# The opening of a fused convolution and MLP: first tile convolved on TensorE by tap diagonals, VectorE's convolution issued ahead by a time budget

## The chip, the cores and the metric

One core of a Trainium2 chip runs the whole kernel. The metric is the device time of one execution in microseconds; the median over the runs counts. TensorE (PE in the profile) multiplies, ScalarE (ACT) applies the silu, VectorE (DVE) convolves and copies results out of PSUM, GpSimd (POOL) and SyncE (SP) issue DMAs.

## What is computed

A causal depthwise convolution of 7 taps over the sequence, whose taps are a softmax over 7 weights of each of 8 heads, feeds a two-layer MLP with a silu that has its own beta for every hidden unit:

```python
batch, seq, d_model = (8, 4096, 192)      # 32768 tokens
kernel_size, n_heads, d_ff = 7, 8, 2048
w = softmax(weight, axis=-1)              # (8, 7)
x_pad = concatenate([zeros((B, 6, D)), x], axis=1)
out = einsum('hk,bskhg->bshg', w, windows of 7 of x_pad, 24 channels a head)
h = out @ w_in                            # (32768, 192) @ (192, 2048)
g = h * (1.0 / (1.0 + exp(-beta * h)))
result = g @ w_out                        # (32768, 2048) @ (2048, 192), float32
```

## The kernel before

The tokens are two streams (`NS = 2`) of 16384 each, four sequences a stream. Stream 0 lies in partitions 0 to 63 of every activation tile, stream 1 in 64 to 127, and the 192 channels are `NK = 3` groups of 64. A step takes the same tokens of both streams. The steps are 128, 128 and 256 tokens (the first tile of 512), and then 31 full tiles of 512.

In a step, `mm1` (L251) makes one of the 16 chunks of 128 hidden units: six matmuls of 64 rows (three channel groups, two streams) into a `ph` tile of PSUM, of which there are two, and one ScalarE activation (L259) that writes `g = silu(beta h)` for both streams. So w_in must lie in both halves of the partitions: `load_w_in` brings each column to one half by a casting DMA from POOL, and `copy_w_in` copies it to the other by a DMA from SP. `mm2` (L285) multiplies the step before: its matmuls of 64 x 192 are set among the `mm1` of this step by `mm2_plan`, gather in two `po` tiles of PSUM, and `store` (L298) copies a finished pair to `o_sb` on VectorE (L301) and writes it out by a DMA from SP. w_out is divided by beta on POOL (L207), because g holds beta h times the sigmoid.

The tokens arrive transposed. `load_x` (L89) brings 128 tokens of one stream a time by a casting DMA from POOL (256 in all), and `transpose_x` (L99) turns a block by a DMA transpose on SP. `conv_ops` (L210) makes for step i+1 a list of a halo copy and 21 VectorE operations (7 taps, 3 groups), one pass over 128 x n each (L229, L231), from the transposed `xt` through a float32 `acc` to the bf16 `xc` that `mm1` reads. The order of the work is written out by hand, each instruction pinned to program order on its engine; the loop takes two of those operations after each `mm1`:

```python
for u in range(NF):
    mm1(i, u)
    for t in plan[u]:
        mm2(i - 1, *t)
    for op in conv[:2]:
        op()
    conv = conv[2:]
```

Step 0 has a path of its own: VectorE multiplies the 128 tokens by each tap (`xw`, L168), and 42 matmuls with a shifted identity add them up (L185). Steps 1 and 2 take the common path.

Of the kernel before, what the change touches and what calls it, by code (L numbers as in the profile page):

```python
# [10 lines left out]
FP32 = mybir.dt.float32  # L11
BF16 = mybir.dt.bfloat16
# [6 lines left out]
def kernel(  # L19
# [9 lines left out]
    nc = tc.nc  # L29
# [4 lines left out]
    group = D // H  # L34
# [3 lines left out]
    NK = D // 64  # L38
    NS = 2
    TS = B * S // NS  # L40
    TILE = 512

# [8 lines left out]
    xbf_pool = ctx.enter_context(tc.tile_pool(name="xbf", bufs=3))  # L51
# [8 lines left out]

    steps = [(0, 128), (128, 128), (256, 256)]
    steps += [(t, TILE) for t in range(TILE, TS, TILE)]
    n_steps = len(steps)


    x0 = consts.tile([128, NS, D], FP32, name="x0")
    pin(nc.sync.dma_start(out=x0, in_=xs[:, 0:128, :].rearrange("s p d -> p s d")))
    wbc = consts.tile([128, H, K], FP32, name="wbc")
    pin(nc.sync.dma_start(out=wbc, in_=weight.rearrange("h k -> (h k)").partition_broadcast(128)))
    beta16 = consts.tile([NF, 128], FP32, name="beta16")  # L70
    pin(nc.sync.dma_start(out=beta16, in_=moe_beta.rearrange("(c p) -> c p", p=128)))

    w_in_s = consts.tile([128, NK, F], BF16, name="w_in_s")
    w_in_v = moe_w_in.rearrange("(k c) f -> c k f", c=64)
# [4 lines left out]
    def load_w_in(half, f0, f1):  # L79
        pin(nc.gpsimd.dma_start(out=w_in_s[64 * half:64 * half + 64, :, f0:f1], in_=w_in_v[:, :, f0:f1]))  # L80

    def copy_w_in(half, f0, f1):
        o = 1 - half
        pin(nc.sync.dma_start(out=w_in_s[64 * o:64 * o + 64, :, f0:f1],
                              in_=w_in_s[64 * half:64 * half + 64, :, f0:f1]))

    xbf_of, xt_of = {}, {}

    def load_x(j, b0=0, b1=4):  # L89
        if j not in xbf_of:  # L90
            xbf_of[j] = xbf_pool.tile([128, 4, NK, NS, 64], BF16, name="x_bf")
        t = xbf_of[j]
        for b in range(b0, b1):
            for s in range(NS):
                src = xs[s, TILE * j + 128 * b:TILE * j + 128 * (b + 1), :]
                pin(nc.gpsimd.dma_start(out=t[:, b, :, s, :],  # L96
                                        in_=src.rearrange("p (k c) -> p k c", c=64)))

    def transpose_x(j, b0=0, b1=4):  # L99
        if j not in xt_of:  # L100
            xt_of[j] = xt_pool.tile([128, NK, LEAD + TILE], BF16, name="xt")
        for b in range(b0, b1):
            c = LEAD + 128 * b
            pin(nc.sync.dma_start_transpose(
                out=xt_of[j][:, :, c:c + 128],
                in_=xbf_of[j][:, b, :, :, :].rearrange("p k s c -> p (k s c)")))


    zeros = consts.tile([128, TILE], BF16, name="zeros")
# [7 lines left out]
    load_w_in(0, 0, 512)  # L117
    load_w_in(1, 0, 512)
    shift = consts.tile([128, 128 + PAD], BF16, name="shift")
    pin(nc.gpsimd.memset(shift, 0.0))  # L120
    pin(nc.gpsimd.affine_select(out=shift, in_=shift, compare_op=ALU.not_equal, fill=1.0,
                                base=PAD, pattern=[[-1, 128 + PAD]], channel_multiplier=1))
    id16 = consts.tile([NF, NF], FP32, name="id16")
    pin(nc.gpsimd.memset(id16, 0.0))
    pin(nc.gpsimd.affine_select(out=id16, in_=id16, compare_op=ALU.not_equal, fill=1.0,
                                base=0, pattern=[[-1, NF]], channel_multiplier=1))
    load_x(0, 0, 4)
    mask = consts.tile([128, NK, H], FP32, name="mask")
    pin(nc.gpsimd.memset(mask, 1.0))
    for s in range(NS):  # L130
        m = mask[64 * s:64 * s + 64, :, :]
        pin(nc.gpsimd.affine_select(out=m, in_=m, compare_op=ALU.is_ge, fill=0.0, base=0,  # L132
                                    pattern=[[64, NK], [-group, H]], channel_multiplier=1))
        pin(nc.gpsimd.affine_select(out=m, in_=m, compare_op=ALU.is_ge, fill=0.0, base=group - 1,  # L134
                                    pattern=[[-64, NK], [group, H]], channel_multiplier=-1))
    load_w_in(0, 512, 1024)
    load_w_in(1, 1024, 1536)
    load_w_in(0, 1536, 2048)
    load_x(1)

    for c in range(0, NF, 4):
        pin(nc.sync.dma_start(out=w_out_f[:, c:c + 4, :], in_=w_out_v[:, c:c + 4, :]))  # L142
        if c == 0:
            transpose_x(0, 0, 2)
            copy_w_in(0, 512, 1024)
        if c == 4:
            copy_w_in(1, 1024, 1536)
            transpose_x(0, 2, 4)
        if c == 8:
            copy_w_in(0, 1536, 2048)  # L150


    mx = consts.tile([128, H], FP32, name="mx")
    pin(nc.vector.tensor_reduce(out=mx, in_=wbc, axis=AX.X, op=ALU.max))
    pin(nc.vector.tensor_tensor(wbc, wbc, mx[:, :, None].to_broadcast([128, H, K]), ALU.subtract))
    pin(nc.scalar.activation(wbc, wbc, AF.Exp))
    pin(nc.scalar.activation(scrap, one, AF.Silu))
    sm = consts.tile([128, H], FP32, name="sm")
    pin(nc.vector.tensor_reduce(out=sm, in_=wbc, axis=AX.X, op=ALU.add))
    rs = consts.tile([128, H], FP32, name="rs")  # L160
    pin(nc.vector.reciprocal(rs, sm))
    taps = consts.tile([128, H, K], FP32, name="taps")
    pin(nc.vector.tensor_tensor(taps, wbc, rs[:, :, None].to_broadcast([128, H, K]), ALU.mult))


    xw = consts.tile([128, K, NS, D], BF16, name="xw")
    for k in range(K):
        pin(nc.vector.tensor_tensor(  # L168
            xw[:, k, :, :].rearrange("p s (h c) -> p s h c", c=group),
            x0.rearrange("p s (h c) -> p s h c", c=group),  # L170
            taps[:, None, :, k:k + 1].to_broadcast([128, NS, H, group]),
            ALU.mult))

    warm = psum_h.tile([128, 2, TILE], FP32, name="ph")
    for i in range(8):
        pin(nc.tensor.matmul(warm[:, i % 2, :], zeros[:, 0:128], zeros, start=True, stop=True))  # L176
    bps = psum_h.tile([128, 2, TILE], FP32, name="ph")
    pin(nc.tensor.transpose(bps[:, 0, 0:NF], beta16, id16))
    cva = psum_o.tile([128, 2, TILE], FP32, name="po")
    cvb = psum_o.tile([128, 2, TILE], FP32, name="po")  # L180
    cv = [cva[:, 0, 0:128], cva[:, 1, 0:128], cvb[:, 0, 0:128]]
    for k in range(K):
        for kk in range(NK):
            for s in range(NS):
                pin(nc.tensor.matmul(cv[kk][64 * s:64 * s + 64, :], xw[:, k, s, 64 * kk:64 * kk + 64],  # L185
                                     shift[:, k:k + 128], start=(k == 0), stop=(k == K - 1)))
    xc_of = {}
    xc_of[0] = xc_pool.tile([128, NK, TILE], BF16, name="xc")
    for kk in range(NK):
        pin(nc.scalar.activation(xc_of[0][:, kk, 0:128], cv[kk], AF.Copy))  # L190

    beta = consts.tile([128, NF], FP32, name="beta")
    pin(nc.vector.tensor_copy(beta, bps[:, 0, 0:NF]))
    rbeta = consts.tile([128, NF], FP32, name="rbeta")
    pin(nc.vector.reciprocal(rbeta, beta))

    tmp3 = consts.tile([128, NK, K, H], FP32, name="tmp3")
    for kk in range(NK):
        pin(nc.vector.tensor_tensor(tmp3[:, kk, :, :],
                                    mask[:, kk:kk + 1, :].to_broadcast([128, K, H]),  # L200
                                    taps.rearrange("p h k -> p k h"), ALU.mult))
    taps3 = consts.tile([128, NK, K], FP32, name="taps3")
    pin(nc.vector.tensor_reduce(out=taps3, in_=tmp3, axis=AX.X, op=ALU.add))


    for c in range(NF):
        pin(nc.gpsimd.tensor_scalar_mul(w_out_s[:, c, :], w_out_f[:, c, :], rbeta[:, c:c + 1]))  # L207


    def conv_ops(i):  # L210
        t0, n = steps[i]
        j, c0 = t0 // TILE, t0 % TILE
        ops = []

        def halo():
            xt = xt_of[j]
            if t0 % S == 0 or t0 == 128:
                pin(nc.vector.memset(xt[:, :, LEAD - PAD:LEAD], 0.0))
            elif c0 == 0:
                pin(nc.vector.tensor_copy(xt[:, :, LEAD - PAD:LEAD], xt_of[j - 1][:, :, TILE + LEAD - PAD:]))  # L220

        def tap(kk, k):
            xt, xc = xt_of[j], xc_of[i]
            acc = accs[i]
            src = xt[:, kk, LEAD - PAD + c0 + k:LEAD - PAD + c0 + k + n]
            w = taps3[:, kk, k:k + 1]
            a = acc[:, kk, 0:n]
            if k == 0:
# [6 lines left out]
        def begin():  # L235
            xc_of[i] = xc_pool.tile([128, NK, TILE], BF16, name="xc")
            accs[i] = acc_pool.tile([128, NK, TILE], FP32, name="acc")
            if c0 == 0 or t0 == 128:
                halo()

        ops.append(begin)
        for k in range(K):
            for kk in range(NK):
                ops.append(lambda kk=kk, k=k: tap(kk, k))
# [133 lines left out]
```

## Time and profile before

| | |
|---|---|
| three runs, median (lowest to highest) | 715.44 us (715.34 to 716.18) |
| the profiled execution | 712.91 us, of which its span is 711.2 us |
| PE busy, share of the span | 687.7 us, 97% |
| ACT, DVE, POOL busy | 578.8, 502.2, 218.2 us |
| mm1 matmuls (L257), mm2 matmuls (L293) | 432.7 us of 3264, 422.4 us of 7936 |
| mean granted TensorE clock | 0.999 |
| DMA over the span | 55.38 MB, 78 GB/s |

The profile is of one execution, so its own time is the one to compare with its span; the median stands 2.5 us above it. Busy times overlap between engines and do not add up to the span, and matmul busy time is that of pipelined instructions. A row of a timeline gives its start, its duration, engine, line, operation, output and input, and in brackets the idle time before it with what ended it.

### The profile page before, as it was taken

To read this page: it belongs to the slowest core of one execution; us is meant where nothing else is said; L and a number is where in the kernel's file an instruction comes from. 1 tells how busy PE (TensorE), PEld (TensorE's weight loads), DVE (VectorE), ACT (ScalarE), POOL (GpSimd) and SP (SyncE) were. 2 spreads that over 40 slices of the span, in tenths; PEclk is the share of its full clock that TensorE was granted. 3 is DMA by queue.
4 is the path that set the end of the run, shared out by engine and by line. 5 is a ranking of instruction groups with operands and counts; after the bars stand their busy time and mean duration, and the time that the engine had idled before them with its cause. 6 is when DMAs were issued, how large, how long until landed. Compare 5 with 4: busy or idle time off the path is not lost.

```text
span 711.2 us, 25346 instructions
## 1 busy us (share of the span) xinstructions
PE 687.7 (97%) x11379; PEld 524.5 (74%) x11379; DVE 502.2 (71%) x877; ACT 578.8 (81%) x552; POOL 218.2 (31%) x290
## 2 busy tenths in 40 slices
PE   5589999999999999999999999999999999999998
PEld 2466777777777777777777777777777777777777
DVE  4779776677687667678667768766776876676702
ACT  3489888888888888888888888888888888888882
POOL 9997332223333113333212333321233330000000
PEclk9999999999999999999999999999999999999999
DMA  9999554455555445555445555544555553221012
GB/s 132 149 95 96 81 88 69 72 84 79 75 80 87 69 73 85 75 72 87 79 71 78 74 74 81 88 71 71 83 80 74 80 85 64 58 62 52 28 44 68
DMA packets 194861, 55.38 MB, mean 78 GB/s; under 512 B 158128, under 2 KB 194752, under 8 KB 194752
## 3 DMA queue, kind: packets, MB, share of 16 engines
q0 software_dynamic: 103440, 13.58, 30.6%
q1 hardware_dynamic: 91312, 40.17, 22.3%
q8 instruction: 89, 1.46, 0.9%
q14 instruction: 20, 0.16, 0.1%
HBM read 28.94 MB, written 25.17 MB: 76 GB/s over the span
## 4 chain that ended last, share of the span: by engine, by line
PE 93%; POOL 2%; DMA 2%; DVE 2%; issue 0%; ACT 0%; SPq 0%; DVEq 0%; POOLq 0%
PE ph L257 46%; PE po L293 46%; PE po L316 2%; DVE acc L231 1%; POOL x_bf L96 1%; DMA w_in_s<-w_in_s 1%; DMA x_bf<-in_x_dram 1%; POOL w_in_s L80 0%; ACT g L259 0%; DVE xc L231 0%; DVE acc L229 0%; SPq L142 0%; POOL mask L132 0%; POOL mask L134 0%; DVE o_sb L320 0%
## 5 line engine op out<-in xcount | busy, mean ns | idle before, releaser
L259 ACT ACTIVATE g<-ph,beta 128x1024 bf16<-128x1024 f32 (+2 forms) x544 | 574.9, 1064 | 111.8 <-PE ph L257 107.4
L257 PE MATMUL ph<-xc,w_in_s 64*128 64x512 bf16 (+2 forms) x3264 | 432.7, 367 | 17.0 <-DMA w_in_s<-w_in_s 9.4
L293 PEld LDWEIGHTS <-g 64*128 64x128 bf16 x7936 | 359.6, 94 | 101.5
L293 PE MATMUL po<-w_out_s,g 64*128 64x192 bf16 x7936 | 422.4, 243 | 0.0
L231 DVE SCALAR_TENSOR_TENSOR acc<-xt,taps,acc 128x512 f32<-128x512 bf16 (+2 forms) x495 | 326.7, 727 | 0.0
L96 POOL DMA_DIRECT2D x_bf<-in_x_dram x256 | 197.5, 774 | 366.7 <-DMA xt<-x_bf 349.4
L257 PEld LDWEIGHTS <-w_in_s 64*128 64x128 bf16 x3264 | 168.2, 96 | 74.6 <-DMA w_in_s<-w_in_s 10.5
L301 DVE COPY o_sb<-po 128x384 f32<-128x384 f32 x124 | 68.9, 556 | 183.5 <-PE po L293 183.5
L231 DVE SCALAR_TENSOR_TENSOR xc<-xt,taps,acc 128x512 bf16<-128x512 bf16 (+2 forms) x99 | 66.5, 727 | 0.0
L229 DVE TENSOR_SCALAR acc<-xt,taps 128x512 f32<-128x512 bf16 (+2 forms) x99 | 41.8, 481 | 9.2 <-DMA xt<-x_bf 8.1
L207 POOL TENSOR_SCALAR w_out_s<-w_out_f,rbeta 128x192 bf16<-128x192 f32 x16 | 15.6, 992 | 0.1
L316 PE MATMUL po<-w_out_s,g 128*128 128x192 bf16 x128 | 10.7, 246 | 0.0
L316 PEld LDWEIGHTS <-g 128*128 128x128 bf16 x128 | 10.5, 98 | 0.2 <-issue 0.2
L320 DVE COPY o_sb<-po 128x192 f32<-128x192 f32 x8 | 2.9, 358 | 7.6 <-PE po L316 7.6
L176 PE MATMUL ph<-zeros 128*128 128x512 bf16 x8 | 3.6, 631 | 1.2 <-DVE one L112 1.2
L220 DVE COPY xt<-xt 128x18 bf16<-128x18 bf16 x28 | 4.6, 166 | 0.0
L185 PE MATMUL po<-shift,xw 128*64 128x128 bf16 x42 | 3.3, 314 | 1.2 <-DVE xw L168 1.2
L185 PEld LDWEIGHTS <-xw 128*64 128x64 bf16 x42 | 2.0, 152 | 2.4 <-DVE xw L168 2.4
L80 POOL DMA_DIRECT2D w_in_s<-in_moe_w_in_dram x5 | 3.3, 665 | 0.8 <-POOLq L362 0.8
L168 DVE TENSOR_TENSOR xw<-x,taps 128x384 bf16<-128x384 f32 x7 | 3.4, 553 | 0.0
L176 PEld LDWEIGHTS <-zeros 128*128 128x128 bf16 x8 | 1.0, 140 | 2.9 <-issue 1.7
L190 ACT ACTIVATE xc<-po 128x128 bf16<-128x128 f32 x3 | 0.6, 278 | 3.1 <-PE po L185 3.1
(30 smaller groups left out, 8.8 us busy)
## 6 DMA issues: line engine op xcount, KB each, us to landing
out_dram<-o_sb SPq DMA_DIRECT2D x124, 192.0 KB, 2.3
x_bf<-in_x_dram POOLq DMA_DIRECT2D x256, 48.0 KB, 3.1
xt<-x_bf SPq DMA_TRANSPOSE x128, 2.3
w_out_f<-in_moe_w_out_dram SPq DMA_DIRECT2D x4, 384.0 KB, 6.7
w_in_s<-in_moe_w_in_dram POOLq DMA_DIRECT2D x5, 192.0 KB, 5.5
out_dram<-o_sb SPq DMA_DIRECT2D x8, 96.0 KB, 1.6
w_in_s<-w_in_s SPq DMA_DIRECT2D x3, 192.0 KB, 6.8
x<-in_x_dram SPq DMA_DIRECT2D x1, 192.0 KB, 2.6
```

Of the source, the lines that this page charges most:

```text
L96: pin(nc.gpsimd.dma_start(out=t[:, b, :, s, :], in_=src.rearrange("p (k c) -> p k c", c=64)))
L176: pin(nc.tensor.matmul(warm[:, i % 2, :], zeros[:, 0:128], zeros, start=True, stop=True))
L185: pin(nc.tensor.matmul(cv[kk][64 * s:64 * s + 64, :], xw[:, k, s, 64 * kk:64 * kk + 64], shift[:, k:k + 128], start=(k == 0), stop=(k == K ...
L207: pin(nc.gpsimd.tensor_scalar_mul(w_out_s[:, c, :], w_out_f[:, c, :], rbeta[:, c:c + 1]))
L220: pin(nc.vector.tensor_copy(xt[:, :, LEAD - PAD:LEAD], xt_of[j - 1][:, :, TILE + LEAD - PAD:]))
L229: pin(nc.vector.tensor_scalar_mul(a, src, w))
L231: pin(nc.vector.scalar_tensor_tensor(out=xc[:, kk, 0:n] if k == K - 1 else a, in0=src, scalar=w, in1=a, op0=ALU.mult, op1=ALU.add))
L257: pin(nc.tensor.matmul(ph[:, s, 0:n], w_in_s[r, kk, ts(fc, 128)], xc_of[i][r, kk, 0:n], start=(kk == 0), stop=(kk == NK - 1)))
L259: pin(nc.scalar.activation(g_of[i][:, fc, :, 0:n], ph[:, :, 0:n], AF.Silu, scale=beta[:, fc:fc + 1]))
L293: pin(nc.tensor.matmul(po[:, q, 0:D], g_of[i][r, fc, s, ts(b, 128)], w_out_s[r, fc, :], start=(phase == 0 and fc == 0), stop=(phase == 1 a ...
L301: pin(nc.vector.tensor_copy(o_sb, po[:, :, 0:D]))
L316: pin(nc.tensor.matmul(po[:, 0, 0:D], g_of[i][:, fc, s, ts(b, 128)], w_out_s[:, fc, :], start=(fc == 0), stop=(fc == NF - 1)))
```

## The change

The tail (`last`) and `mm1` and `mm2` of the full steps stay as they are. These parts differ:

- **Channels.** Channel c now belongs to group c mod 3 (`(q k)` instead of `(k c)`), so the 64 lanes of every group carry the same heads, 8 lanes each, and one tap scalar a partition serves all three groups (`tapn`).
- **Taps.** They are loaded as 8 x 7 and spread over 128 partitions by a matmul with a 0/1 selector; the softmax is done there, and its division goes into the scaling of the results (`rsum`).
- **First tile.** Its four blocks of 128 tokens are loaded as float32, transposed on TensorE, and convolved there: seven diagonal matrices, one a tap, are the weights, in float32r. The diagonal matrix of a half is repeated over all 128 output columns, so both halves of the partitions get the channels of one stream. Results are scaled into `xcp0` to `xcp2`.
- **mm1 of the first tile** (`mm1_pair`). As each half has both streams, the halves compute different hidden chunks, u and u + 8, and need w_in only where it was loaded. The copies to the other half come later, from POOL, for the full-tile path.
- **w_out** is loaded from POOL and divided by beta on VectorE (`scale_w_out`), among the steps 0 and 1.
- **x of the later tiles.** Loaded as float32, four blocks a DMA, from SP (the second tile from POOL); cast by VectorE (`cast_x`; half of the second tile by POOL), and then transposed as before.
- **Steps.** The tiles 1 to 3 are taken as six steps of 256 tokens; the convolution of a 256-step handles the three groups in one operation.
- **Order on VectorE.** Casts, transposes, loads and convolutions of all later steps stand in one list. After each chunk `vector_work` issues from it as much as a budget of time allows (1307 ns a full chunk, 560 less for each o_sb copy), at most two steps ahead, and at the end of a step at least all of the next one.

In the instruction streams, TensorE goes from 22,759 rows to 22,992, POOL keeps 19 DMAs and two casts in all, and SP has per full tile four transposes, two loads and four stores.

```diff
-    NK = D // 64
+    NK = 3
+    Q = D // NK
...
-    xbf_pool = ctx.enter_context(tc.tile_pool(name="xbf", bufs=3))
+    xf_pool = ctx.enter_context(tc.tile_pool(name="xf", bufs=2))
+    xbf_pool = ctx.enter_context(tc.tile_pool(name="xbf", bufs=2))
...
-    steps += [(t, TILE) for t in range(TILE, TS, TILE)]
+    NP = len(steps)
+    steps += [(t, 256) for t in range(TILE, 4 * TILE, 256)]
+    steps += [(t, TILE) for t in range(4 * TILE, TS, TILE)]
...
+    def cast_x(j, s, b0=0, b1=NB, eng=None):
...
+        pin((eng or nc.vector).tensor_copy(
+            xbf_of[j][:, b0:b1, :, s, :].rearrange("p b k q -> p k b q"),
+            xf_of[j][:, b0:b1, s, :].rearrange("p b (q k) -> p k b q", k=NK)))
...
+    for f in range(0, HF, 512):
+        for s in range(NS):
+            load_w_in(s, HF * s + f, HF * s + f + 512)
+        if f == 0:
+            load_x0(1)
+    load_x0(2)
+    for c in range(0, NF, 4):
+        pin(nc.gpsimd.dma_start(out=w_out_f[:, c:c + 4, :], in_=w_out_v[:, c:c + 4, :]))
+        if c == 0:
+            load_x0(3)
+    for b in (0, 2):
+        for s in range(NS):
+            load_x(1, s, b, b + 2, nc.gpsimd)
+    for f in range(0, HF, 512):
+        for s in range(NS):
+            copy_w_in(s, HF * s + f, HF * s + f + 512)
+    for s in range(NS):
+        cast_x(1, s, 2, 4, nc.gpsimd)
...
+    pin(nc.scalar.activation(etap, tap_ps, AF.Exp, bias=nmax, accum_out=tsum))
+    diag = consts.tile([128, K, NS, Q], FP32R, name="diag")
+    for k in range(K):
+        pin(nc.vector.tensor_scalar_mul(diag[:, k, :, :], ident2, etap[:, k:k + 1]))
...
+    def transpose_0(bank, b):
...
+        for kk in range(NK):
+            pin(nc.tensor.transpose(t[:, kk, :], v[:, kk, :], ident))
...
+    def conv_0(cv, b, k0=0, k1=K):
+        for k in range(k0, k1):
+            for s in range(NS):
+                pin(nc.tensor.matmul(
+                    cv[:, s, 0:NK * 128], diag[half_of(s), k, :, :].rearrange("p s q -> p (s q)"),
+                    xr[b][half_of(s), :, k:k + 128], start=(k == 0), stop=(k == K - 1)))
...
+    def mm1_pair(i, u):
...
+        fcs = (u, u + NF // 2)
+        for kk in range(NK):
+            for h in range(2):
+                pin(nc.tensor.matmul(ph[:, h, 0:NS * n], w_in_s[half_of(h), kk, ts(fcs[h], 128)],
+                                     xc_of[i][half_of(h), :, kk, :],
+                                     start=(kk == 0), stop=(kk == NK - 1)))
+        for h in range(2):
+            pin(nc.scalar.activation(g_of[i][:, fcs[h], :, 0:n],
...
+    def fetched(j):
+        for b in range(NB):
+            transpose_x(j, b)
+        if (j + 2) * TILE < TS:
+            for s in range(NS):
+                load_x(j + 2, s)
...
+    def vector_work(i, ns, flush=False):
+        nonlocal budget
+        budget += ns
+        while work and ((budget > 0 and work[0][0] <= i + 2) or (flush and work[0][0] <= i + 1)):
+            budget -= work[0][1]
+            work.pop(0)[2]()
+        budget = min(budget, 0.0) if work else 0.0
...
+            for u in range(NF // 2):
+                mm1_pair(0, u)
+                if u == 0:
+                    t = transpose_0(po01[:, 1, :], 1)
+                    take_0(t, 1)
+                    halo_0(t, 1)
+                elif u == 1:
+                    cv = po_tile()
+                    conv_0(cv, 1)
+                    for s in range(NS):
+                        evac_0(cv, 1, s, nc.vector)
...
+                if u >= 4:
+                    for c in range(2 * (u - 4), 2 * (u - 3)):
+                        scale_w_out(c)
...
+                if i == 2:
+                    if u == 0:
+                        for s in range(NS):
+                            cast_x(1, s, 0, 2)
+                        for b in range(NB):
+                            transpose_x(1, b)
+                        for s in range(NS):
+                            load_x(3, s)
+                    else:
+                        vector_work(i, 1300, flush=u == NF // 2 - 1)
```

## The prediction

> **What bounds the kernel now.** I read the busy shares first, then the 40 slices, then a table of windows, then the waits of the first 60 us, last the timeline there.
>
> ```profile
> PE 687.7 (97%) x11379; PEld 524.5 (74%) x11379; DVE 502.2 (71%) x877; ACT 578.8 (81%) x552; POOL 218.2 (31%) x290
> ...
> PE   5589999999999999999999999999999999999998
> ```
>
> TensorE is the bound, and full everywhere but in the first slices (17.8 us each). The windows split this:
>
> ```profile
> 20.00:30.00 10.00, 4.46 (x59) 2.94 (x60) 6.00 (x16) 3.71 (x9) 10.00 (x11) 1.00 1.60 205
> 50.00:60.00 10.00, 6.92 (x88) 4.25 (x90) 9.96 (x18) 6.18 (x7) 9.94 (x13) 1.00 1.19 103
> 300.00:320.91 20.91, 20.91 (x354) 16.01 (x352) 15.42 (x26) 17.82 (x17) 6.16 (x8) 1.00 0.52 78
> ```
>
> Columns are length, then busy PE, PEld, DVE, ACT, POOL, then granted clock, DMA share, GB/s. A full 512-token step takes 20.91 us with PE busy throughout and DVE at 15.4: nothing that the change does to DVE or DMA can shorten it. The opening is another stage, and its waits (total, times, longest) name the limits:
>
> ```profile
> ACT g L259 <- PE ph L257: 18.9, 15, 8.1
> PE ph L257 <- DMA w_in_s<-w_in_s: 9.4, 3, 5.7
> DVE acc L229 <- DMA xt<-x_bf: 8.1, 2, 4.1
> PE ph L257 <- DVE xc L231: 3.1, 3, 2.6
> PE ph L257 <- DMA w_in_s<-in_moe_w_in_dram: 2.1, 1, 2.1
> ```
>
> The copies of w_in to the other half and the DMA transposes are late, then DVE's convolution of the first full tile. The timeline dates it:
>
> ```profile
> 1.25 3.60 PE L176 MATMUL ph<-zeros 128*128 128x512 bf16 x8 [1.25 <-DVE one L112]
> 11.59 0.84 ACT L259 ACTIVATE g<-ph,beta 128x256 bf16<-128x256 f32 x2 [0.38 <-PE ph L257]
> 34.06 0.56 PE L257 MATMUL ph<-xc,w_in_s 64*128 64x128 bf16 x6
> 34.61 0.34 PE L257 MATMUL ph<-xc,w_in_s 64*128 64x128 bf16 x6
> 40.31 10.22 ACT L259 ACTIVATE g<-ph,beta 128x512 bf16<-128x512 f32 x16 [0.24 <-PE ph L257]
> 41.81 10.01 DVE L231 SCALAR_TENSOR_TENSOR acc<-xt,taps,acc 128x512 f32<-128x512 bf16 x15
> 52.54 0.39 PE L257 MATMUL ph<-xc,w_in_s 64*128 64x512 bf16 x2 [2.57 <-DVE xc L231]
> 54.35 6.17 ACT L259 ACTIVATE g<-ph,beta 128x1024 bf16<-128x1024 f32 x6 [3.82 <-PE ph L257]
> ```
>
> ScalarE starts on the first tile at 11.59 and on the second only at 54.35, though its work between is 32 x 0.42 + 10.22 = 23.7 us. From 54.35 to the end are 656.85 us: a first full step at 16.3 us (16 activations at a pitch of 1.017), 30 steps of 20.91, and 13.25 of last stage and store. What can be won lies before 54.35, about 30 us with a perfect opening.
>
> **The change, part by part.**
>
> *After 54.35.* Three 512-steps become six 256-steps. On PE a 256-slot is half of 1.307, 0.654 us; ScalarE's 16 activations of 128x512 took 10.22, 0.639 each. They are nearly level, and the ph pool has two buffers, so each mm1 waits for the activation two before; I take 0.67 (bounds 0.65 and 0.75). The rest is 96 x 0.67 + 16.3 + 27 x 20.91 + 13.25 = 658.4, or 1.6 us more than now (bounds 0 and 9).
>
> *Steady DVE and queues.* The x loads leave POOL (256 issues, 197.5 us, hidden already: worth nothing) for SP: two per tile at 0.45 each beside four transposes at 1.22 and four stores at 0.37, 7.3 of 20.91 us. SP is in order: a transpose now waits for DVE's cast, and loads and stores queue behind it; four o_sb buffers and two xf buffers cover that, a store being needed only four evacuations later. DVE gains two casts per tile. The nearest row is the TENSOR_SCALAR 128x512 at 0.46 a piece (384.39, 1.28 for three); 768 elements at that rate are 0.6, at the 0.667 us pace of the two-input taps 0.93. [...] By the row DVE is at 15.4 + 2 x 0.75 = 16.9 per tile[...], and two steps of lead absorb an evacuation in between. Cost on the path: 0 (bounds 0 and 2).
>
> *First silu.* The wbc broadcast, xw and shift go; an fp32 selector matmul, three fp32 transposes of x0, seven diagonals on DVE and 14 float32r matmuls of 384 columns come. Taps land near 3.4 (0.80 + 2.6, the x row), selector matmul and maximum and exp to 4.5 (rows 0.26, 0.21, 0.25 and signals), seven diagonals of 0.25 to 6.3, transposes and ScalarE's copy of 384 (0.5) to 6.2. The matmul has no row: as one pass at the 0.43 us per 512 of the warm-up it is 0.32 a pair, 2.3 a block[...]. I take one pass, since the bf16 rows are the nearest[...]. Scaling into xc 0.55, first mm1 0.6 and signals (ScalarE's own x0 issue, 0.46, and its silu table, 1.28, fall in its waits): first silu at 10.2 (bounds 8.7 and 17), now 11.59.
>
> *Steps 0 and 1.* w_in copies are gone from the path, because each half holds other F columns and both halves get both token streams. ScalarE needs 6.7 us a step; PE carries mm1, three blocks of transposes and three of convolution besides. By the early rows (0.43 per 512 columns; the six mm1 at 34.06) step 0 would take PE 5.1 + 3 + 4.6 = 12.7; by the late pace (0.34 at 34.61) 6.7. The granted clock reads 1.00 in both. [...] I take 8.0 for step 0. Step 1 has mm1, one block and 64 mm2 (2.6): 7.5. It ends at 25.7. The scaling of w_out moves from POOL (16 x 0.99, beside other work) to DVE: between the pitches of TENSOR_SCALAR at 128 and 256 columns (0.25 and 0.42) I take 0.33, 5.3 us; with six scalings of xc and three copies of x at 0.55 and the halos DVE has 10.8 of the 15.5 us to do. It waits there in order for each part of w_out, and behind that wait stand the copy and the scaling of the last 128 tokens, which PE needs early in step 1 and ScalarE in step 2: covered as long as w_out is on time. The POOL queue has 19 transfers before the casts; the order of instructions shows each waiting for the one eight before it, and two casts of tile 1 follow them on POOL (128x384; at twice the 0.99 of its 128x192 row they end near 21). With the 6 us landing of now, w_out's last part comes near 17, and x of tile 1 near 17, against needs at 20 and 25.7.
>
> *Tile 1.* Its casts stand on DVE behind the o_sb of step 0, which is ready when step 1 ends. From there: o_sb 0.56, two half casts 1.1; on SP a store and two loads until +2.0, two transposes 2.4, landing 2.3 (median) to 5.7 (opening) after issue: +6.7. The 256 convolution is 0.6 + 6 x 0.93 = 6.2, then mm1 to silu 0.6: 13.5 us (bounds 11.5 and 16), more than the 10.2 of step 2, so ScalarE still waits some 3 us. The second tile starts at 39.2. After it DVE needs 8 to 9 us per 256-step of 10.7, so its lead grows.
>
> *Sum.* 54.35 - 39.2 = 15.15, less 1.6, is 13.5 us. The profiled execution of 712.91 (span 711.2) would become 699.4 (span 697.7). The median of the runs, 715.44, stands 2.5 above the profiled one; from it 702.
>
> **The rivals.**
>
> *Transfers arrive late.* Now 1.60 of DMA share at 20 to 30 and landings up to 7.9 speak for it, larger rows against. At 12 us a landing the first x0 block of POOL's ring would free w_out's last load at 15 and that would land at 27, 7 to 8 us after PE needs it: 710. Chance 0.09.
>
> *256-slots are held by ScalarE's round trip.* At 0.75 a slot 96 slots cost 9.2 instead of 1.6: 709.5. For it: ScalarE at 0.639 against 0.654; against: step 2 of now kept 0.64. Chance 0.05.
>
> *Slower: [...].* Place: the four blocks in the opening, in PE's order ahead of mm1. Price: the cold block 9 instead of 2.3, three warm ones 4.5 instead of 1.3 or so, together 16: 718. It decides from about 5 us a block, where the 13.5 are spent. For it: no float32r row[...]. Against: operands are rounded to this type just for it. Chance 0.07. DVE as bound needs casts over 2.7 us; 0.02, on the same side.
>
> *It does not do what it says*: the lead of DVE cannot show where PE is the bound; so if the opening stays at 54, no difference. Chance 0.03.
>
> **How the numbers follow.** The main case has the remaining 0.74 and spans 694 (all lower bounds: first silu 8.7, steps 6.7 each, chain 11.5) to 707. The range 693 to 711 takes in the two slow but faster cases[...]. About 0.2% (1.4 us) is what a measurement can tell. Faster: 0.74 + 0.09 + 0.05 = 0.88; same 0.03; slower 0.09.
>
> **What would show it.** Steady steps at 20.91 and DVE near 17 in them; silu of step 0 near 10; the 128x384 matmuls at 0.16 to 0.32 a pair; the first tap of tile 1 near 32 and a PE wait on DVE xc of about 3 us; 256-slots at 0.65 to 0.68. Wrong if the 512-step changes length, if PE waits for w_out_s in step 1, or if a block takes over 4 us.

## The result and the profile after

The changed kernel takes 704.42 us (median; 704.16 to 705.64) against 715.39: ratio 0.985, 95% interval 0.983 to 0.987. That is 11.0 us less; 13.5 were forecast, 702 in the range 693 to 711. The profiled executions differ by less, 712.91 to 704.65 (spans 711.2 and 702.9), because the one of before stood 2.5 us under its median and the one of after 0.2 over.

The profile page of the kernel after, its busy shares and the TensorE row of the slices:

```profile
PE 689.8 (98%) x11561; PEld 542.6 (77%) x11561; DVE 541.4 (77%) x901; ACT 587.4 (84%) x600; POOL 15.9 (2%) x29
...
PE   8879999999999999999999999999999999999998
```

The weak slices at the start have become 8, 8 and 7 instead of 5 and 5. The windows (length, then busy PE, PEld, DVE, ACT, POOL, granted clock, DMA share, GB/s):

```profile
300.00:320.91 20.91, 20.91 (x356) 16.03 (x352) 16.96 (x29) 17.83 (x17) 0.00 (x0) 1.00 0.41 100
...
40.00:50.00 10.00, 6.91 (x114) 6.61 (x116) 9.75 (x12) 4.88 (x8) 0.00 (x0) 0.83 0.31 83
```

A full step is 20.91 us as before, with VectorE at 16.96 of it instead of 15.42 and POOL idle. What is left lies in the window from 40 on, and before it. The waits of the first 60 us (total, times, longest):

```profile
ACT g L302 <- PE ph L298: 6.9, 6, 2.1
...
DVE acc L279 <- DMA xt<-xb: 5.4, 1, 5.4
...
PE ph L311 <- DVE xc L281: 5.0, 1, 5.0
...
PE ph L175 <- DVE beta L240: 1.3, 1, 1.3
```

And the timeline of the same stretch (start, length, engine, line, operation, how many in a row; in brackets the wait ahead of the first and what ended it):

```profile
6.08 0.48 PE L175 MATMUL ph<-zeros 128*128 128x128 bf16 x3 [1.35 <-DVE beta L240]
6.49 2.61 PE L217 MATMUL ph<-xr,diag 64*128 64x384 f32 x14
...
11.38 0.84 ACT L302 ACTIVATE g<-ph,beta 128x256 bf16<-128x256 f32 x2 [1.66 <-PE ph L298]
...
17.14 1.53 PE L217 MATMUL po<-xr,diag 64*128 64x384 f32 x14
...
29.02 0.56 DVE L356 COPY o_sb<-po 128x384 f32<-128x384 f32 x1 [3.27 <-PE po L348]
29.49 0.90 DVE L84 CAST xb<-xf 128x384 bf16<-128x384 f32 x2
29.73 9.37 ACT L302 ACTIVATE g<-ph,beta 128x512 bf16<-128x512 f32 x16 [0.28 <-PE ph L298]
31.18 5.18 SPq L95 DMA_TRANSPOSE xt<-xb  x4
...
35.86 0.75 DVE L279 TENSOR_SCALAR acc<-xt,tapn 128x768 f32<-128x768 bf16 x1 [5.40 <-DMA xt<-xb]
36.65 5.24 DVE L281 SCALAR_TENSOR_TENSOR acc<-xt,tapn,acc 128x768 f32<-128x768 bf16 x5
...
43.09 0.82 PE L311 MATMUL ph<-xc,w_in_s 64*128 64x256 bf16 x6 [5.02 <-DVE xc L281]
44.33 0.69 ACT L314 ACTIVATE g<-ph,beta 128x512 bf16<-128x512 f32 x1 [5.24 <-PE ph L311]
...
46.49 61.96 ACT L314 ACTIVATE g<-ph,beta 128x512 bf16<-128x512 f32 x94 [0.57 <-PE ph L311]
```

ScalarE starts on tile 1 at 44.33 instead of 54.35, 10.0 us earlier; from there to the end are 658.6 us instead of 656.85. The difference, 8.3, is that of the two spans. The chain in front of 44.33 is readable line by line: the o_sb copy of step 0 at 29.02, casts, transposes from 31.18, taps from 35.86, the first matmul at 43.09, 5 us after TensorE ran dry.

The gain stands in steps 0 and 1: step 2 begins at 29.73 instead of 40.31, 10.6 us earlier, and from there to the silu of tile 1 it is 14.6 us instead of 14.0. The waits of TensorE for w_in, 9.4 and 2.1 us in the kernel before, are no longer among the waits. That the parts which took them away (w_in used where it was loaded, the first tile convolved on TensorE) are the cause is read from these rows; no run put one of them back, so their shares are not separated.

### The profile page after: what moved, and what is told of

It reads as the page before. It is cut to its first block, busy times and chain, and to the rows that moved or that the text cites. A ratio compares the mean times of both kernels' runs of the same rounds, so it can differ in the third digit from the quotient of the medians.

```text
span 702.9 us, 25421 instructions
## 1 busy us (share of the span) xinstructions
PE 689.8 (98%) x11561; PEld 542.6 (77%) x11561; DVE 541.4 (77%) x901; ACT 587.4 (84%) x600; POOL 15.9 (2%) x29
## 4 chain that ended last, share of the span: by engine, by line
PE 94%; DMA 2%; DVE 2%; POOL 1%; SPq 0%; issue 0%; ACT 0%; POOLq 0%; DVEq 0%
PE po L348 46%; PE ph L311 46%; PE po L371 2%; DMA w_in_s<-in_moe_w_in_dram 1%; DMA xf<-in_x_dram 1%; DVE acc L281 1%; DMA xt<-xb 0%; PE ph L298 0%; POOL w_in_s L110 0%; PE po L217 0%; POOL xf L78 0%; DVE w_out_s L255 0%; SPq L95 0%; DVE xc L281 0%; SPq L78 0%
## 5 line engine op out<-in xcount | busy, mean ns | idle before, releaser
L314 ACT ACTIVATE g<-ph,beta 128x1024 bf16<-128x1024 f32 (+1 forms) x544 | 561.0, 1039 | 89.7 <-PE ph L311 86.0
L311 PE MATMUL ph<-xc,w_in_s 64*128 64x512 bf16 (+1 forms) x3264 | 420.3, 358 | 5.0 <-DVE xc L281 5.0
L281 DVE SCALAR_TENSOR_TENSOR acc<-xt,tapn,acc 128x512 f32<-128x512 bf16 (+1 forms) x450 | 315.3, 763 | 0.9
L311 PEld LDWEIGHTS <-w_in_s 64*128 64x128 bf16 x3264 | 168.9, 94 | 51.6 <-issue 5.2
L281 DVE SCALAR_TENSOR_TENSOR xc<-xt,tapn,acc 128x512 bf16<-128x512 bf16 (+1 forms) x90 | 64.2, 763 | 0.2
L84 DVE CAST xb<-xf 128x768 bf16<-128x768 f32 (+1 forms) x62 | 48.9, 826 | 0.0
L279 DVE TENSOR_SCALAR acc<-xt,tapn 128x512 f32<-128x512 bf16 (+1 forms) x90 | 40.5, 501 | 6.5 <-DMA xt<-xb 5.4
L302 ACT ACTIVATE g<-ph,beta 128x256 bf16<-128x256 f32 (+1 forms) x48 | 22.0, 564 | 7.4 <-PE ph L298 6.9
L298 PE MATMUL ph<-xcp,w_in_s 64*128 64x256 bf16 (+1 forms) x144 | 15.2, 320 | 2.1 <-ACT g L302 1.4
L298 PEld LDWEIGHTS <-w_in_s 64*128 64x128 bf16 x144 | 7.2, 98 | 6.2 <-issue 4.2
L371 PEld LDWEIGHTS <-g 128*128 128x128 bf16 x128 | 10.5, 98 | 0.2 <-issue 0.2
L217 PE MATMUL po<-xr,diag 64*128 64x384 f32 x42 | 5.7, 415 | 0.6 <-DVE xr L208 0.6
```

The costliest lines, as they stand in the source:

```text
L84: pin((eng or nc.vector).tensor_copy(xbf_of[j][:, b0:b1, :, s, :].rearrange("p b k q -> p k b q"), xf_of[j][:, b0:b1, s, :].rearrange("p b ...
L217: pin(nc.tensor.matmul(cv[:, s, 0:NK * 128], diag[half_of(s), k, :, :].rearrange("p s q -> p (s q)"), xr[b][half_of(s), :, k:k + 128], sta ...
L279: pin(nc.vector.tensor_scalar_mul(a, src, w))
L281: pin(nc.vector.scalar_tensor_tensor(out=xc_of[i][:, k0:k1, 0:n] if k == K - 1 else a, in0=src, scalar=w, in1=a, op0=ALU.mult, op1=ALU.add))
L298: pin(nc.tensor.matmul(ph[:, h, 0:NS * n], w_in_s[half_of(h), kk, ts(fcs[h], 128)], xc_of[i][half_of(h), :, kk, :], start=(kk == 0), stop= ...
L302: pin(nc.scalar.activation(g_of[i][:, fcs[h], :, 0:n], ph[:, h, 0:NS * n].rearrange("p (s t) -> p s t", s=NS), AF.Silu, scale=beta[:, fcs[ ...
```

## The experiments

Unless it says otherwise an edit is made to the changed kernel; times are medians, to be set against 704.42 for it and 715.4 for the kernel before (715.4 to 715.6 beside every group of runs). TensorE reached its full rate (a block of diagonals in 1.5 us instead of 2.6) at different moments in different executions (last section), so that with the same opening step 2 began anywhere from 26.4 to 30.1 us; where profiles are compared, distances from the start of step 2 say more than the times themselves.

### What holds tile 1

**Casts, transposes and loads of tile 1 earlier.**

```diff
                 if i == 2:
                     if u == 0:
-                        for s in range(NS):
-                            cast_x(1, s, 0, 2)
-                        for b in range(NB):
-                            transpose_x(1, b)
                         for s in range(NS):
                             load_x(3, s)
...
+                if i == 1 and u == 2:
+                    for s in range(NS):
+                        cast_x(1, s, 0, 2)
+                    for b in range(NB):
+                        transpose_x(1, b)
+                    for s in range(NS):
+                        load_x(2, s)
-            if i == 1:
-                for s in range(NS):
-                    load_x(2, s)
```

> The casts and transposes of tile 1 are issued in the third pair of step 1 instead of at the start of step 2, ahead of the first o_sb copy, and tile 2's loads follow the transposes on SP. Opening theory (the end is set by when ScalarE starts on tile 1, now 44.33 us into the span, held by the chain o_sb, casts, two loads, transposes, taps from 29.0): the taps start near 31.5 instead of 35.9 and end near 38.6, before step 2 ends at 39.1, so the silu of tile 1 starts near 39.4: 5 us less, and near 1 more because TensorE no longer idles 5 us and slows: 698 to 700 against 704.4. Rival (transfers of x bound the opening: x of tile 1 is late and only hidden): taps still start after 34, gain under 2 us.

Measured: 697.25 us (ratio 0.975, 0.974 to 0.976 to the kernel before), 7.2 less than the changed kernel and just under the 698 to 700 expected. Its timeline:

```profile
10.52 0.50 PE L298 MATMUL ph<-xcp,w_in_s 64*128 64x256 bf16 x6 [0.71 <-DVE xcp L228]
28.05 9.35 ACT L302 ACTIVATE g<-ph,beta 128x512 bf16<-128x512 f32 x16 [0.28 <-PE ph L298]
37.84 14.48 ACT L314 ACTIVATE g<-ph,beta 128x512 bf16<-128x512 f32 x22 [0.44 <-PE ph L311]
```

From the start of step 2 to the silu of tile 1 it is now 9.8 us (14.6 before the edit), little more than the activations of step 2, and the short steps run at their pace from the first slot. So x of tile 1 had been there in time; it was the order of the work, the casts on VectorE behind an o_sb copy that waits for the end of step 1 and the transposes on SP behind a store and two loads, that cost 4.8 us. The span fell by 7.4: besides the 4.8, TensorE's slow restart is gone (0.9), and in this execution step 2 also began 1.7 us earlier (TensorE's rate, below).

**Only the loads behind the transposes on SP.** `load_x(2, s)` moves from the end of step 1 to behind the transposes of tile 1.

> Only the order on SP: the two loads of tile 2 are issued after the four transposes of tile 1. Opening theory: the first transpose is issued 1.1 us earlier (30.1 instead of 31.2) and has no 786 KB load beside it, so its landing falls from 3.3 to about 2.3: 1 to 2 us less, 702.5 to 703.4. Rival (the cast on VectorE holds the transposes): 0.

Measured: 701.92 us (0.982, 0.980 to 0.983), 2.5 less, a little more than expected.

```profile
28.25 5.19 SPq L95 DMA_TRANSPOSE xt<-xb  x4
32.10 0.75 DVE L279 TENSOR_SCALAR acc<-xt,tapn 128x768 f32<-128x768 bf16 x1 [3.80 <-DMA xt<-xb]
40.23 1.26 ACT L314 ACTIVATE g<-ph,beta 128x512 bf16<-128x512 f32 x2 [3.32 <-PE ph L311]
```

From the first transpose to the first tap 3.9 us instead of 4.7, and from step 2 (27.56 here) to the silu of tile 1 12.7 instead of 14.6. Two loads of 384 KB ahead of the transposes on SP cost 1.9 us of the 14.6. That distance does not depend on when TensorE changed its rate: it is 14.6 to 14.7 in three more profiles that leave this part alone (one step of lead, two short steps, casts along rows). The span of this execution fell by 3.6: the 1.9, and 2.2 because step 2 began earlier, less 0.5 behind it. How much of the median's 2.5 is due to the edit beyond the 1.9 is not shown.

### What holds the first silu

**Without the three idle matmuls.** The line `warm(3, 128)` between the transposes and the first diagonal matmul is left out.

> Leaves out the three idle matmuls on zeros between the transposes of x0 and the first diagonal matmul; they wait for VectorE's copy of beta until 6.08 us, behind seven diagonals. Opening theory with PE's order as the limit: the first diagonal matmul starts near 5.1 instead of 6.49, the first silu near 10.1 instead of 11.38, and everything behind moves by 1.0 to 1.4 us: 703.0 to 703.4. Rival (from step 0 on the transfers of w_in, w_out and x are the limit): the first silu moves, the start of tile 1 does not, 0.

Measured: 703.51 us (0.983, 0.981 to 0.984), 0.9 less.

```profile
5.10 2.61 PE L217 MATMUL ph<-xr,diag 64*128 64x384 f32 x14 [0.37 <-ACT xr L206]
27.99 9.35 ACT L301 ACTIVATE g<-ph,beta 128x512 bf16<-128x512 f32 x16 [0.28 <-PE ph L297]
42.84 0.69 ACT L313 ACTIVATE g<-ph,beta 128x512 bf16<-128x512 f32 x1 [5.50 <-PE ph L310]
```

The first diagonal starts 1.4 us earlier, and so does the first silu, at 9.99. The idle matmuls wrote a PSUM tile whose other half VectorE's copy of beta still had to read, and that copy stands behind seven diagonals. Whether anything of it reaches tile 1 is not shown. Its silu moves from 44.33 to 42.84, but in this execution TensorE also reached its full rate earlier than in that of the kernel after, within the second block of diagonals. The version with two short steps (below) kept the idle matmuls, began step 2 at 28.06, and was at tile 1 just as soon:

```profile
28.06 9.35 ACT L302 ACTIVATE g<-ph,beta 128x512 bf16<-128x512 f32 x16 [0.28 <-PE ph L298]
42.73 0.69 ACT L314 ACTIVATE g<-ph,beta 128x512 bf16<-128x512 f32 x1 [5.32 <-PE ph L311]
```

The timed gain, 0.9, is not clear of noise either (the two intervals overlap).

**Both together.**

> The early casts and the missing idle matmuls together. Opening theory: 5 to 6 and 1.2 add up, 697 to 699. Rival: with the taps early, the next wait is for x of tile 1 or for w_out in step 1, and only the larger of the two gains is left.

Measured: 696.45 us (0.974, 0.972 to 0.975), 0.8 less than the early casts alone and just under the 697 to 699 expected; the 0.8 is not clear of noise.

```profile
11.44 2.54 PE L217 MATMUL po<-xr,diag 64*128 64x384 f32 x14
38.71 13.83 ACT L313 ACTIVATE g<-ph,beta 128x512 bf16<-128x512 f32 x21 [1.03 <-PE ph L310]
```

The second block of diagonals took 2.54 us here and 1.5 in the execution of the early casts: with that, step 2 began at 28.33, 0.3 later than there. How soon TensorE goes from the slow to the full rate (a block of diagonals from 2.6 to 1.5 us) hides what leaving out the idle matmuls brought, and whether the two gains add up stays open.

**No gaps on TensorE.** To the version with both edits, matmuls on zeros in the two gaps that were left.

```diff
+    for _ in range(4):
+        pin(nc.tensor.matmul(cv0[:, 0, 0:128], zeros[:, 0:128], zeros[:, 0:128], start=True, stop=True))
     conv_0(cv0, 0)
...
-    warm(6, 128)
+    warm(12, 128)
```

> The kernel with early casts and without the three idle matmuls, with matmuls on zeros in the two remaining gaps of TensorE (four ahead of the first diagonal matmul, written to its own PSUM tile, and twelve instead of six behind it). If an uninterrupted stretch brings full rate, the second block of diagonals takes 1.5 us instead of 2.5 in every execution and step 2 starts at 26 to 27 instead of 28.3: 694 to 695.5 against 696.4. If the moment of the switch is set by something else, 696 to 697.

Measured: 695.52 us (0.972, 0.970 to 0.975), six runs from 695.03 to 696.28.

```profile
10.95 1.53 PE L217 MATMUL po<-xr,diag 64*128 64x384 f32 x14 [0.22 <-DVE xr L208]
35.94 24.37 ACT L315 ACTIVATE g<-ph,beta 128x512 bf16<-128x512 f32 x37 [0.15 <-ACT g L303]
```

Step 2 began at 26.42 and there is no wait in front of tile 1. The 0.9 to the version without the filling is not clear of noise, and one profile at full rate proves little, since two versions with the gaps, early casts and only the loads, showed a second block as short in theirs (1.52 and 1.51). Whether the filling moves the switch stays open; the best median of this study, 8.9 us under the changed kernel, is this version's.

### What the lead and the short steps are worth

**One step of lead instead of two**: `work[0][0] <= i + 2` becomes `i + 1`.

> VectorE may run one step ahead instead of two. Theory that the lead matters where 256-steps turn to 512-steps: the first 512 convolution can then only begin when the last 256-step begins; casts 1.6, 21 operations 13.4 and two o_sb copies 1.1 make 16.1 us against a step of 10.55, so TensorE waits 5 to 6 us at about 108 us into the span: 709 to 711. Rival (TensorE is the bound after the opening, so the lead buys nothing): 704.0 to 704.8.

Measured: 717.50 us (1.003, 1.002 to 1.005), 13.1 more than the changed kernel and slower than the kernel before.

```profile
115.45 1.11 ACT L314 ACTIVATE g<-ph,beta 128x1024 bf16<-128x1024 f32 x1 [6.92 <-PE ph L311]
...
128.03 0.56 DVE L356 COPY o_sb<-po 128x384 f32<-128x384 f32 x1 [5.83 <-PE po L348]
...
137.11 1.11 ACT L314 ACTIVATE g<-ph,beta 128x1024 bf16<-128x1024 f32 x1 [4.24 <-PE ph L311]
```

The wait at the first 512-step came where it was reckoned and somewhat longer (6.9 against 5 to 6), and a second followed. The first full step is short, because the mm2 beside it are half as many (16.3 us in the kernel before), about as long as VectorE's 17 us of work for the next tile; and VectorE stood idle for 5.8 us in it, as an o_sb copy came ahead of eleven of the 21 taps in its order. The expectation had stopped at the first wait and so missed by 6.5 us. The rival, that the lead buys nothing, falls.

**Tiles 1 to 3 as full steps.** The 256-steps are left out; the casts of tile 2 stand behind the first convolution, as the transposed tile 1 comes first. With the short steps goes the operation over three groups, which only they use.

```diff
-    steps += [(t, 256) for t in range(TILE, 4 * TILE, 256)]
-    steps += [(t, TILE) for t in range(4 * TILE, TS, TILE)]
+    steps += [(t, TILE) for t in range(TILE, TS, TILE)]
...
```

> Tiles 1 to 3 are taken as 512-steps again. Theory that the first convolution is the wait: taps run from 35.9 for 13.9 us instead of 7.1, so the silu of tile 1 starts near 51.2 instead of 44.3; three full steps instead of six halves give 1.7 back, and the next convolution with its casts (17.7) is longer than the first full step (16.3): 709 to 711. Rival (256-steps cost in ScalarE's round trip what they bring): 703 to 705.

Measured: 720.13 us (1.007, 1.006 to 1.009), 15.7 more.

```profile
52.13 1.11 ACT L313 ACTIVATE g<-ph,beta 128x1024 bf16<-128x1024 f32 x1 [14.85 <-PE ph L310]
...
74.39 1.11 ACT L313 ACTIVATE g<-ph,beta 128x1024 bf16<-128x1024 f32 x1 [4.90 <-PE ph L310]
```

ScalarE idles 14.85 us for the first convolution and 4.90 for the second, with smaller waits at 76.9 and 79.1. The direction and the first wait were right (52.1 against 51.2), the second one and the slow restart after each (2.50 and 2.20 us between silus after the second, 1.31 later) were under-reckoned, and the time came out 9 us above the range.

**Only tile 1 as short steps**: `4 * TILE` becomes `2 * TILE` in both lines.

> Only tile 1 is taken as two 256-steps, tiles 2 and 3 as 512-steps. The silu of tile 1 stays near 44.3. Theory that VectorE needs several short steps to get ahead: the convolution of tile 2 ends near 69 when TensorE wants it at 65.5, a wait of 3 to 5 us there: 707 to 709. Rival (only the first tile matters): 703.5 to 704.5.

Measured: 707.00 us (0.989, 0.987 to 0.990), 2.6 more.

```profile
67.80 1.11 ACT L314 ACTIVATE g<-ph,beta 128x1024 bf16<-128x1024 f32 x1 [3.39 <-PE ph L311]
```

The wait is where and as long as reckoned. So of the six short steps the first two bring most (13.1 of the 15.7), and the other four 2.6.

**Short steps alone, in the kernel before.** Its step list becomes that of the changed kernel, with `elif i > 2 and steps[i][0] % TILE == 0:` ahead of the loads.

> The kernel before with the step list of the changed one (tiles 1 to 3 as six 256-steps) and nothing else; each group still has its own operation. Theory that short steps need the merged operation: the first half of tile 1 is convolved in 10.1 us, so its silu starts near 51.4 instead of 54.35, but VectorE then needs 10.1 + 0.6 to 1.1 us per step of 10.5 and the six halves lose 1.7: 713 to 717 against 715.5. Rival (short steps alone are the gain): 705 to 711.

Measured: 715.54 us (1.001, 0.999 to 1.002): no difference.

```profile
40.83 73.54 ACT L260 ACTIVATE g<-ph,beta 128x512 bf16<-128x512 f32 x112 [0.16 <-PE ph L258]
117.96 1.11 ACT L260 ACTIVATE g<-ph,beta 128x1024 bf16<-128x1024 f32 x1 [3.59 <-PE ph L258]
...
42.37 6.01 DVE L232 SCALAR_TENSOR_TENSOR acc<-xt,taps,acc 128x256 f32<-128x256 bf16 x15
...
50.53 0.56 DVE L302 COPY o_sb<-po 128x384 f32<-128x384 f32 x1 [0.96 <-PE po L294]
```

The 112 activations of step 2 and of all six short steps follow without a break, so the wait in front of tile 1 is gone; it comes back at the first full step, at 114.4, because VectorE has saved nothing up: its convolution for that step runs from 104.1 to 117.4. The reason given in the expectation was wrong, though. A short step's convolution took 8.2 us (41.34 to 49.5) and not 10.1, so that VectorE had time to spare in each of the six and waited 1.0 to 1.6 us for an o_sb copy; with one step of lead its order has nothing else to put there. Together with the run of one step of lead this says that the short steps pay only if VectorE may use them to get ahead. That it also needs the merged operation for this is not shown; no run gave the kernel before more lead.

### The slower rival, and the cast

**Diagonals in float32**: the type of `diag` and `xr` is `float32` instead of `float32r`.

> Diagonals and first-tile tokens are float32 instead of float32r, nothing else; this is the slower rival of the prediction. If [...], the first block grows from 2.6 to about 10 us and the three others from 1.5 to 2.6 to about 6, all ahead of mm1 in TensorE's order: 16 to 21 us more than the changed kernel, 720 to 725. If weight loads or signals set the pace of a block, it stays under 710.

Measured: 718.01 us (1.004, 1.003 to 1.005), 13.6 more and a little under the 720 to 725 expected.

```profile
6.49 6.50 PE L217 MATMUL ph<-xr,diag 64*128 64x384 f32 x28
22.61 4.80 PE L217 MATMUL po<-xr,diag 64*128 64x384 f32 x28
```

Each matmul has become two, and a pair of those takes 4.80 / 14 = 0.34 us where one float32r pair takes 1.53 / 7 = 0.22. A block costs 4.8 instead of 1.5 at full rate, 3.1 times as much: the rival is real, at 13.6 us instead of the 16 that was its author's estimate, and only the type keeps it away.

**Casts along rows.** The read `(q k)` becomes `(k q)`, consecutive channels; the later tiles then meet weights in another channel order.

> The casts read their 768 elements with consecutive channels instead of every third, so the channels of the later tiles stand in another order than their weights; only the casts' time is looked at. If [...], a cast falls from 0.80 to about 0.5 us; if not, it stays at 0.80. The kernel's time does not move by more than 0.5 us in either case, as the casts lie beside other work.

Two casts in a full step, with the edit first, and in the changed kernel:

```profile
310.97 1.27 DVE L84 CAST xb<-xf 128x768 bf16<-128x768 f32 x2
```

```profile
313.21 1.60 DVE L84 CAST xb<-xf 128x768 bf16<-128x768 f32 x2
```

0.64 against 0.80 us a cast: the stride of 12 bytes costs a quarter, less than the expected fall to 0.5 would have meant. The one time, 702.43, is 2 under the changed kernel's median, but in it TensorE reached its full rate earliest of all (step 2 at 26.37), so this single execution says nothing on the sum.

## Why the prediction was right

**The bound and the place.** Right: full steps stayed at 20.91, and all that was gained lies ahead of tile 1. The part behind it was put at 658.4 and is 658.6: 96 short slots from 44.33 to 108.80, 0.672 a slot against 0.67, but not quite as thought, since they run at 0.659 (61.96 over 94) and a slow restart adds the rest.

**First silu**: 11.38 instead of 10.2. The diagonals started at 6.49 instead of 6.3, and their block took 0.3 more than reckoned. The largest term is a second scaling into xc: one stream is scaled on ScalarE and the other on VectorE, and the prediction counted one, 0.55, but VectorE began only when ScalarE was done:

```profile
9.75 0.62 DVE L228 TENSOR_SCALAR xcp<-ph,rsum 128x384 bf16<-128x384 f32 x1 [3.76 <-ACT xcp L226]
```

That TensorE stood behind the copy of beta was not seen. Without those idle matmuls the first silu came at 9.99.

**Step 0**: 9.9 us (11.38 to about 21.2) instead of 8.0, **step 1** 8.5 instead of 7.5. The prediction took 8.0 from between 12.7 at the early pace and 6.7 at the late one; when TensorE would reach full rate was its author's estimate. In the profiled execution of after that came near 15.5, in that of the early casts near 10, with the same instructions up to there. A block of diagonals was put at 2.3 slow and 1.3 fast, and took 2.61 and 1.53. Step 1 does not hang on the rate, as it also took some 8.4 with the early casts: there the fourth block of diagonals stands in TensorE's order, it waited for VectorE's copy of x, and ScalarE waited for it.

```profile
21.74 1.51 PE L217 MATMUL po<-xr,diag 64*128 64x384 f32 x14 [0.56 <-DVE xr L208]
...
23.64 5.81 ACT L302 ACTIVATE g<-ph,beta 128x256 bf16<-128x256 f32 x14 [1.55 <-PE ph L298]
```

**Tile 1**: 14.6 us instead of 13.5. The term mis-sized is the price of a tap on 768 elements, 1.05 instead of 0.93 (5.24 for five), 0.9 over seven operations; in proportion to the 0.667 of 512 elements, which the prediction names, it would have been 1.00. The landing of the transposes, taps 6.8 after the o_sb copy against 6.7, was right. A wait of TensorE of 3 us had been expected, and it was 5.0, followed by three slots at half pace: the first mm1 from 43.09 to 46.2 come every 1.28 us, later every 0.66. So from the last tap to the silu it took 1.4 us instead of 0.6; that the sum is not larger is because the o_sb copy came 0.7 before the start of step 2.

**The sum.** These four are 1.2, 1.9, 1.0 and 1.1 us, 5.2 together, which is the gap between the profiled 704.65 and the 699.4 forecast for it: on the profiled executions 8.3 of the 13.5 us came. Some 1.7 of the 5.2 belong to the late change of rate in this one execution. The median came out only 2.4 off, because the two profiled executions stand differently to their medians; that part of the agreement is chance.

**The lead.** The prediction was wrong on why it matters. Under its last rival it said that the lead of DVE cannot show where PE is the bound. TensorE is the bound only as long as VectorE has saved up enough: without the second step of lead the kernel is 13.1 us slower, at the change of step length, a place for which the prediction had no term. "Its lead grows" was right, and it took all six short steps: VectorE's first wait for TensorE after 60 us is at 87.

**The rivals.** Late transfers: not on the path; the early casts found x there, and the waits of the opening name no w_out on TensorE, though POOL's cast waited for its part of x until 20.3, where 17 was reckoned. Short slots at 0.75: no, 0.66. Slow diagonals: 718 was forecast, on block times that were the author's estimate, and 718.0 is what the float32 run takes, but by chance, 13.6 above 704.4 instead of 16 above 702. The casts cost what the prediction took from the row: VectorE's 16.96 us per full step agrees with its 16.9, and a quarter of a cast's consecutive price, 0.80 against 0.64 us, is what the stride added.

## What to carry to other kernels

Where one engine is full for most of the span, ask what it costs that engine to start, and follow the chain to its first full step link by link: a copy that waits, and what is queued behind it, was worth 4.8 us here. An engine that is not the bound still needs a stock of finished work wherever the length of the steps changes; reckon its work against each step, not against the mean, and test the lead by taking it away. Change step length and lead together: in the kernel before, shorter steps alone did nothing, although VectorE had time to spare in them.

## What the runs showed of the hardware that was not expected

- The same instructions ran at two rates, and the change came at very different moments. The six matmuls of the first mm1 took 0.82 us in the profile of after and 0.50 in that of the early casts. In the seven profiles with this same opening step 2 began at 26.37 us (casts along rows), at 27.56 to 28.06 (four) and at 29.73 and 30.05 (the kernel after, and one step of lead). By TensorE's rows the full pace was there at 6.33 in the first of these, at 10.5 with the early casts and with only the loads moved, where the first block had still taken 2.61 us, and near 15.5 in the kernel after, whose second block took 2.61 and whose third took 1.53. In the earliest, the first block of diagonals already took 1.50 us instead of 2.61:

```profile
6.33 1.50 PE L217 MATMUL ph<-xr,diag 64*128 64x384 f32 x14
```

The granted clock of the kernel after reads 1.00 from 6 to 15.5 us as well as from 15.5 to 20. The moments lie some 9 us apart (6.33 to 15.5), and what sets them is not shown. TensorE's two gaps of 1.35 and 0.67 us in this opening may be part of it; the version without gaps left it open.
- After an idle stretch of 5.02 us in the middle TensorE ran at half pace for about 3 us more (43.09 to 46.2, a short slot in 1.28 us instead of 0.66), and there the granted clock does fall: to 0.83 in the window of 10 us, to 0.50 in the stretch itself.

```profile
43.00:46.20 3.20, 3.11 (x34) 2.85 (x36) 3.17 (x5) 1.37 (x2) 0.00 (x0) 0.50 0.11 36
```

With only the loads moved ScalarE waited 3.32 us for TensorE, the first two silus came at full pace (1.26 us for both), and of the next the starts at 41.83, 43.11 and 44.22 lie 1.28 and 1.11 apart; with early casts and no idle matmuls it waited 1.03 us, and the 21 silus behind it took 13.83, 0.66 each. The waits of 5.02 and 3.32 us cost more than their length.
- A pair of float32r matmuls of 64 x 384, side by side on the two halves of the rows, came every 0.22 us at full rate (1.53 / 7). The six matmuls of mm1 in a full step, 512 columns each, take 0.65 us to the start of the mm2 behind them, 0.217 a pair, so that 384 columns at their pace would be 0.16. The weight load of the float32r matmul takes 0.184 us in the trace; whether it sets the pace is not shown, as no run took it away.
- VectorE's taps on 256 elements took 0.49 us each in the kernel before (7.34 for fifteen), all of them while POOL scaled w_out, and 0.40 in the short steps of the same code, when POOL had finished that (6.01 for fifteen, above):

```profile
19.47 15.63 POOL L207 TENSOR_SCALAR w_out_s<-w_out_f,rbeta 128x192 bf16<-128x192 f32 x16
...
26.74 7.34 DVE L231 SCALAR_TENSOR_TENSOR acc<-xt,taps,acc 128x256 f32<-128x256 bf16 x15
```

That POOL's work is what slowed them is read from the overlap; no run took it away alone.
- A tap on the three groups at once (768 elements) took 1.05 us, where three operations of 256 take 1.20 beside no work of POOL: 13% less. A line through 0.40 at 256 and 0.667 at 512 gives the 0.93 of the prediction for 768; why the operation over three groups takes 0.12 more stays open.
